# Gated linear attention followed by a maxout MoE: inputs of batches 1 to 3 loaded by one DMA per tensor and batch

## The chip, the cores and the metric

One core of one Trainium2 chip. The metric is the device time of one execution in microseconds (us). Each version ran several times; a run of the kernel before went with every group, on the same chip. Runs over 1.5% above the fastest run of the same kernel are set aside as slow; only fast runs are compared.

Engines go by the profile's names: PE is the tensor engine (matmuls), DVE the vector engine, ACT the scalar engine, POOL the GpSimd engine, SP the one that issues the input loads. The granted clock is the share of its full clock that PE was given, 1.00 at full clock.

## The reference

Two parts, cut to what matters here. Shapes: batch 4, 8 heads, sequence 768, head size 48, all in fp32.

```python
def _attn_ref(q, k, v, alpha):
    ...
    for t in range(S):
        state = alpha[:, :, t, :, None] * state + np.einsum('bhd,bhe->bhde', k[:, :, t], v[:, :, t])
        y[:, :, t] = np.einsum('bhd,bhde->bhe', q[:, :, t], state)
def _moe_ref(x, w1, w2, w_out):               # w1, w2: 384 x 1024, w_out: 1024 x 384
    h1 = x @ w1
    h2 = x @ w2
    g = np.maximum(h1, h2)
    return (g @ w_out).astype(np.float32)
# x is y with heads side by side: (batch * sequence, heads * head size) = 3072 x 384
```

## The kernel before

The sequence of each batch is cut into 6 chunks of 128 rows, so there are 24 chunks, 6 per batch. Chunk 6 is the first of batch 1, chunk 12 the first of batch 2, chunk 18 the first of batch 3. Each chunk needs four inputs of 192 KB (alpha, k, q, v: 128 partitions, 8 heads, 48 values of 4 bytes), and each came by its own DMA, two chunks ahead in the program:

```python
ldp = ctx.enter_context(tc.tile_pool(name="ldp", bufs=8))
def load(i):
    b, c = divmod(i, NCH)                     # NCH = 6, C = 128
    t = {}
    for name, src in (("af", alpha), ("kf", k), ("qf", q), ("vf", v)):
        t[name] = ldp.tile([128, H, D], FP32, tag=name, name=name)
        nc.sync.dma_start(out=t[name], in_=src[b, :, c * C : (c + 1) * C, :].rearrange("h p d -> p h d"))
    loads[i] = t
```

The chain of one chunk, by the names that the profile shows (`...` marks cuts):

```python
lg = Ln(af)                # ACT        vp = cast(vf)          # POOL
cs = mrec @ lg             # PE: decay sums
Em, Ep = exp(-cs), exp(cs) # ACT
kn = kf * Em               # POOL       qn = qf * Ep           # DVE
tp = transposes of kn, qn  # PE, 4 + 4  qk = copy(tp)          # DVE
kv = kn^T @ vp             # PE, 4      tm, sb: state          # DVE, POOL
pp = qk @ qk               # PE, 8      pt = pp * mask         # DVE
yp = sb, vp products       # PE, up to 16
...
# moe(w), for each window of two chunks, one window behind:
hp = w12 @ xt              # PE, 24     gT = relu(hp)          # ACT, DVE
op = w2o @ xt + wo @ gT    # PE, 22     outs -> DRAM           # ACT queue
```

The MoE matmuls (hp, op) do not depend on the chunk in work. (As max(h1, h2) is h2 + relu(h1 - h2), w12 holds w1 - w2, and w2o holds w2 times w_out, wo.) They are the filler for the holes that the chain leaves on the tensor engine. The program's scheduler fixes the order of each engine's instructions when the program is built; it decides by its own estimate of when the data will be there.

Of the kernel before, what the change touches and what calls it, by code (L numbers as in the profile page):

```python
# [9 lines left out]
FP32 = mybir.dt.float32  # L10
# [5 lines left out]
def kernel(  # L16
# [20 lines left out]
    nc = tc.nc  # L37
    B, H, S, D = q.shape
    C = 128
    NCH = S // C  # L40
    NI = B * NCH
    HP = H // 2
    P64 = 64
    NT, DM = out.shape
    DFF = moe_w1.shape[1]
    NF = DFF // 128
    ND = DM // 128
# [2 lines left out]

    constp = ctx.enter_context(tc.tile_pool(name="constp", bufs=1))
    wp = ctx.enter_context(tc.tile_pool(name="wp", bufs=1))
    ldp = ctx.enter_context(tc.tile_pool(name="ldp", bufs=8))
    gp = ctx.enter_context(tc.tile_pool(name="gp", bufs=3))
    mp = ctx.enter_context(tc.tile_pool(name="mp", bufs=2))
    psp = ctx.enter_context(tc.tile_pool(name="psp", bufs=1, space=bass.MemoryType.PSUM))

    nc.scalar.preload_act_table_set("natural_log_exp_and_others")

    loads = {}  # L60

    def load(i):
        b, c = divmod(i, NCH)
        t = {}
        for name, src in (("af", alpha), ("kf", k), ("qf", q), ("vf", v)):
            t[name] = ldp.tile([128, H, D], FP32, tag=name, name=name)
            nc.sync.dma_start(out=t[name], in_=src[b, :, c * C : (c + 1) * C, :].rearrange("h p d -> p h d"))
        loads[i] = t

    load(0)  # L70
    load(1)
    w2f = wp.tile([128, ND, DFF], FP32)
    wof = wp.tile([128, NF, DM], FP32)
    w1f = wp.tile([128, ND, DFF], FP32)
    nc.sync.dma_start(out=w2f, in_=moe_w2.rearrange("(s p) f -> p s f", p=128))
    nc.sync.dma_start(out=wof, in_=moe_w_out.rearrange("(s p) d -> p s d", p=128))
    nc.sync.dma_start(out=w1f, in_=moe_w1.rearrange("(s p) f -> p s f", p=128))
# [17 lines left out]
    for n in range(NB):  # L95
        for lst, nm in ((LG, "lg"), (QN, "qn"), (KN, "kn")):
            t = constp.tile([128, H, P64], FP16, name=f"{nm}{n}")
            nc.gpsimd.memset(t, 0.0)
            lst.append(t)
        t = constp.tile([128, 128 + H * VS], FP16, name=f"vp{n}")  # L100
# [3 lines left out]
    for n in range(3):  # L104
        t = constp.tile([128, 128 + HP * SS], FP16, name=f"sb{n}")
# [20 lines left out]
    def weights():  # L126
        for ds in range(ND):
            nc.scalar.copy(out=w2h[:, ds, :], in_=w2f[:, ds, :])
            wt = psp.tile([128, NF, 128], FP16, tag="m", bufs=3, name="wt")
            for f in range(NF):  # L130
                nc.tensor.transpose(wt[:, f, :], w2h[:, ds, f * 128 : (f + 1) * 128], ident)
            nc.vector.tensor_copy(out=w2T[:, :, ds * 128 : (ds + 1) * 128], in_=wt)
        nc.gpsimd.tensor_copy(out=wo16, in_=wof)
        for ds in range(ND):
            wq = psp.tile([128, DM], FP32, tag="m", bufs=3, name="wq")
            for f in range(NF):
                nc.tensor.matmul(
                    wq, lhsT=w2T[:, f, ds * 128 : (ds + 1) * 128], rhs=wo16[:, f, :],
                    start=(f == 0), stop=(f == NF - 1),
                )  # L140
            nc.scalar.copy(out=w2o[:, ds, :], in_=wq)
        for ds in range(ND):
            nc.vector.tensor_sub(out=w12[:, ds, :], in0=w1f[:, ds, :], in1=w2f[:, ds, :])
# [3 lines left out]

    def gla(i):
        b, c = divmod(i, NCH)
        t = loads.pop(i)  # L150
        lg, qn, kn, vp = LG[i % NB], QN[i % NB], KN[i % NB], VP[i % NB]
        vd = vp[:, 128:].rearrange("p (h w) -> p h w", w=VS)[:, :, 0:D]
        nc.scalar.activation(out=lg[:, :, 0:D], in_=t["af"], func=ACTF.Ln)
# [31 lines left out]
        if c:  # L185
# [5 lines left out]
            for a in range(2):  # L191
# [3 lines left out]
                    out=sd[r, :, e], in0=tm[r], in1=dd[r, :].unsqueeze(2).to_broadcast([64, HP, D])  # L195
# [24 lines left out]
        for a in range(2):  # L220
            nc.vector.tensor_mul(  # L221
                out=pt[:, a], in0=pa[a], in1=u16.unsqueeze(1).to_broadcast([128, HP, C])
# [10 lines left out]
        w = i // 2  # L233
# [4 lines left out]
    def moe(w):  # L238
        xt = xts.pop(w)
        gT = mp.tile([128, NF, 2 * C], FP16, tag="gT", name="gT")  # L240
        for f2 in range(NF // 2):
            hp = psp.tile([128, 2, 2 * C], FP32, tag="m", bufs=3, name="hp")
            for n in range(2):
                f = 2 * f2 + n
                for ds in range(ND):
                    nc.tensor.matmul(  # L246
                        hp[:, n, :], lhsT=w12[:, ds, f * 128 : (f + 1) * 128],
                        rhs=xt[:, ds].rearrange("p n t -> p (n t)"), start=(ds == 0), stop=(ds == ND - 1),
                    )
            if f2 % 2 == 0:  # L250
                nc.scalar.activation(out=gT[:, 2 * f2 : 2 * f2 + 2, :], in_=hp, func=ACTF.Relu)  # L251
            else:
                nc.vector.tensor_relu(out=gT[:, 2 * f2 : 2 * f2 + 2, :], in_=hp)  # L253
        outs = mp.tile([128, 2, DM], FP32, tag="outs", bufs=3, name="outs")
        for n in range(2):
            op = psp.tile([128, DM], FP32, tag="m", bufs=3, name="op")
            for ds in range(ND):
                nc.tensor.matmul(op, lhsT=xt[:, ds, n, :], rhs=w2o[:, ds, :], start=(ds == 0), stop=False)  # L258
            for f in range(NF):
                nc.tensor.matmul(  # L260
                    op, lhsT=gT[:, f, n * C : (n + 1) * C], rhs=wo16[:, f, :], start=False, stop=(f == NF - 1)
                )
            nc.scalar.copy(out=outs[:, n, :], in_=op)  # L263
        nc.scalar.dma_start(
            out=out[w * 2 * C : (w + 1) * 2 * C, :].rearrange("(n p) d -> p n d", p=C), in_=outs
        )

    LAG = 1
    NWIN = NI // 2
    for i in range(NI):  # L270
        if i + 2 < NI:
            load(i + 2)
        gla(i)
        if i == 1:
            weights()
        if i % 2 == 1 and i // 2 - LAG >= 0:
            moe(i // 2 - LAG)
    for w in range(NWIN - LAG, NWIN):
        moe(w)
# [30 lines left out]
```

## Time and profile before

| | kernel before |
|---|---|
| time, median of the three runs at hand then | 187.52 us (187.39 to 189.44) |
| span of the profiled execution | 185.5 us |
| packets of inputs | 98,304 of 192 B |
| mean granted clock of the tensor engine, profiled execution | 0.990 |

The page and its main rows stand in the prediction below. Two more rows: the slices of the page (40 of 4.64 us; a digit is the busy share in tenths) for the tensor engine and for its granted clock.

```profile
PE   0025779779887898896997878888878988969991
PEclk9999969999999999999999999999999999999999
```

The clock row has a 6 in slice 6, and is full (9) elsewhere. Read the same kernel in stretches of 3.41 us from 61 to 74.65 us; 3.41 us is the step in which the recorded clock changes in these traces (the kernel before: 0.50 from 24.66 to 28.07). (Columns: stretch, its length, busy time of PE with instructions, granted clock, mean share of the DMA engines, GB/s. A share over 1 means that the recorded times of packets overlap.)

```profile
61.00:64.41 3.41, 3.41 (x41) 1.00 0.58 116
64.41:67.83 3.42, 2.85 (x31) 1.00 1.41 195
67.83:71.24 3.41, 3.38 (x36) 1.00 1.15 154
71.24:74.65 3.41, 2.71 (x30) 1.00 1.06 256
```

Where batch 1 begins, PE is busy between 79% (2.71 of 3.41) and 100%, at full clock.

### The profile page before, as it was taken

The numbers are of one execution on the slowest core, as the hardware profiler recorded it, in microseconds if no ns is written. First come the engines' busy times: TensorE is split into PE (matmuls) and PEld (weight loads), VectorE is DVE, ScalarE is ACT, GpSimd is POOL, SyncE is SP. The second block draws the span as 40 slices with busy tenths as digits, with TensorE's granted clock in tenths as the row PEclk, the third lists the DMA queues.
The fourth block names the chain that finished last, engine by engine and source line by source line (L and its number), as shares of the span: only waits on it lengthen the run. The fifth ranks groups of instructions, "written<-read, shape, count | busy, mean of one in ns | idle before, by whom it ended". The sixth has DMA issues, their size and how long they took to land. (4 is left out here: it accounts for less than half of the span.)

```text
span 185.5 us, 3954 instructions
## 1 busy us (share of the span) xinstructions
PE 145.4 (78%) x1544; PEld 101.6 (55%) x1544; DVE 102.6 (55%) x175; ACT 73.8 (40%) x175; POOL 75.9 (41%) x129
## 2 busy tenths in 40 slices
PE   0025779779887898896997878888878988969991
PEld 0024637556555666564675555566556665646760
DVE  4122765782764962955926757717649529559220
ACT  3306306525454616426344443252455163253331
POOL 8950730661464245436512543523633353355000
PEclk9999969999999999999999999999999999999999
DMA  6999999999699599996999994997920020020022
GB/s 119 189 351 378 370 189 169 196 187 168 163 201 216 114 191 206 190 189 142 185 161 221 205 208 105 194 189 157 169 88 0 4 85 2 5 85 0 4 85 85
DMA packets 104963, 28.57 MB, mean 154 GB/s; under 512 B 100080, under 2 KB 104176, under 8 KB 104944
## 3 DMA queue, kind: packets, MB, share of 16 engines
q1 hardware_dynamic: 101680, 23.60, 73.7%
q10 hardware_dynamic: 3264, 4.72, 7.4%
q8 instruction: 12, 0.20, 0.5%
q14 instruction: 7, 0.06, 0.1%
HBM read 23.59 MB, written 4.72 MB: 153 GB/s over the span
## 5 line engine op out<-in xcount | busy, mean ns | idle before, releaser
L171 POOL TENSOR_TENSOR kn<-kf,Em 128x384 f16<-128x384 f32 x24 | 23.9, 995 | 79.2 <-ACT Em L167 59.4
L260 PE MATMUL op<-wo,gT 128*128 128x384 f16 x192 | 40.6, 326 | 0.0
L246 PE MATMUL hp<-xt,w 128*128 128x256 f16 x288 | 38.9, 272 | 1.7 <-ACT xt L236 1.1
L221 DVE TENSOR_TENSOR pt<-pp,u 128x512 f16<-128x512 f32 x48 | 30.9, 685 | 6.2 <-PE pp L219 5.7
L253 DVE TENSOR_SCALAR gT<-hp 128x512 f16<-128x512 f32 x24 | 16.4, 684 | 24.1 <-PE hp L246 24.0
L246 PEld LDWEIGHTS <-w 128*128 128x128 f16 x288 | 26.1, 97 | 5.9 <-issue 3.2
L172 DVE TENSOR_TENSOR qn<-qf,Ep 128x384 f16<-128x384 f32 x24 | 21.1, 878 | 14.1 <-ACT Ep L168 10.6
L232 PE MATMUL yp<-pt,vp 128*128 128x128 f16 x240 | 26.3, 223 | 1.1 <-DVE pt L221 0.8
L177 PE MATMUL tp<-ident,kn 128*128 128x128 f16 x96 | 10.7, 229 | 19.5 <-POOL kn L171 19.5
L263 ACT COPY outs<-op 128x384 f32<-128x384 f32 x24 | 11.5, 480 | 33.6 <-PE op L260 33.5
L181 DVE COPY qk<-tp 128x1024 f16<-128x1024 f16 x24 | 16.5, 689 | 14.3 <-PE tp L177 12.9
L260 PEld LDWEIGHTS <-gT 128*128 128x128 f16 x192 | 16.9, 97 | 9.9 <-issue 1.8
L251 ACT ACTIVATE gT<-hp 128x512 f16<-128x512 f32 x24 | 14.4, 602 | 18.3 <-PE hp L246 18.2
L194 POOL TENSOR_TENSOR sb<-tm,dd 64x192 f16<-64x192 f32 x40 | 20.3, 506 | 2.9
L177 PEld LDWEIGHTS <-kn 128*128 128x128 f16 x96 | 6.1, 100 | 26.0 <-POOL kn L171 26.0
L232 PEld LDWEIGHTS <-vp 128*128 128x128 f16 x240 | 18.2, 100 | 3.3 <-issue 0.2
L167 ACT ACTIVATE Em<-cs 128x384 f32<-128x384 f32 x24 | 11.8, 493 | 18.8 <-PE cs L161 18.8
L236 ACT CAST xt<-yp 128x384 f16<-128x384 f32 x24 | 11.5, 479 | 18.6 <-PE yp L232 17.3
L154 POOL CAST vp<-vf 128x384 f16<-128x384 f32 x24 | 13.1, 550 | 12.6 <-PE yp L232 9.1
L232 PE MATMUL yp<-qk,sb 128*128 128x128 f16 x120 | 16.8, 222 | 1.0 <-POOL sb L194 1.0
L258 PE MATMUL op<-w2o,xt 128*128 128x384 f16 x72 | 16.9, 325 | 0.0
L209 DVE TENSOR_TENSOR tm<-kv,sb 64x192 f32<-64x192 f32 x32 | 11.3, 352 | 5.7 <-POOL sb L194 5.0
(46 smaller groups left out, 161.4 us busy)
## 6 DMA issues: line engine op xcount, KB each, us to landing
af<-in_alpha_dram SPq DMA_DIRECT2D x24, 192.0 KB, 4.5
kf<-in_k_dram SPq DMA_DIRECT2D x24, 192.0 KB, 4.6
qf<-in_q_dram SPq DMA_DIRECT2D x24, 192.0 KB, 4.6
vf<-in_v_dram SPq DMA_DIRECT2D x24, 192.0 KB, 4.6
out_dram<-outs ACTq DMA_DIRECT2D x12, 384.0 KB, 3.4
w2f<-in_moe_w_dram SPq DMA_DIRECT2D x1, 1536.0 KB, 7.3
wof<-in_moe_w_out_dram SPq DMA_DIRECT2D x1, 1536.0 KB, 10.5
w1f<-in_moe_w_dram SPq DMA_DIRECT2D x1, 1536.0 KB, 14.0
```

Of the source, the lines that this page charges most:

```text
L171: nc.gpsimd.tensor_mul(out=kn[:, :, 0:D], in0=t["kf"], in1=Em)
L172: nc.vector.tensor_mul(out=qn[:, :, 0:D], in0=t["qf"], in1=Ep)
L177: nc.tensor.transpose(tp[:, n, j, :], src[:, 2 * j : 2 * j + 2, :].rearrange("p h w -> p (h w)"), ident)
L181: nc.vector.tensor_copy(out=qk, in_=tp)
L194: nc.gpsimd.tensor_mul(out=sd[r, :, e], in0=tm[r], in1=dd[r, :].unsqueeze(2).to_broadcast([64, HP, D]))
L221: nc.vector.tensor_mul(out=pt[:, a], in0=pa[a], in1=u16.unsqueeze(1).to_broadcast([128, HP, C]))
L232: nc.tensor.matmul(yp[:, ds, :], lhsT=l, rhs=r, start=(n == 0), stop=(n == len(mms) - 1))
L246: nc.tensor.matmul(hp[:, n, :], lhsT=w12[:, ds, f * 128 : (f + 1) * 128], rhs=xt[:, ds].rearrange("p n t -> p (n t)"), start=(ds == 0), st ...
L251: nc.scalar.activation(out=gT[:, 2 * f2 : 2 * f2 + 2, :], in_=hp, func=ACTF.Relu)
L253: nc.vector.tensor_relu(out=gT[:, 2 * f2 : 2 * f2 + 2, :], in_=hp)
L258: nc.tensor.matmul(op, lhsT=xt[:, ds, n, :], rhs=w2o[:, ds, :], start=(ds == 0), stop=False)
L260: nc.tensor.matmul(op, lhsT=gT[:, f, n * C : (n + 1) * C], rhs=wo16[:, f, :], start=False, stop=(f == NF - 1))
```

## The change

The intent: fewer and longer DMAs. Batch 0 is still loaded by chunks, because the first chunk should start early. For batches 1 to 3 there is one DMA per tensor and batch (1.1 MB). Each head's 48 values go to a slot of 64 values (256 B). Two buffers per tensor hold whole batches; the fp32 weights are staged in the same buffers, and one buffer of the working tiles is given up for the room (gp, three to two). The whole change:

```diff
--- before.py
+++ after.py
@@ -50,28 +50,36 @@
 
     constp = ctx.enter_context(tc.tile_pool(name="constp", bufs=1))
     wp = ctx.enter_context(tc.tile_pool(name="wp", bufs=1))
-    ldp = ctx.enter_context(tc.tile_pool(name="ldp", bufs=8))
-    gp = ctx.enter_context(tc.tile_pool(name="gp", bufs=3))
+    ldp = ctx.enter_context(tc.tile_pool(name="ldp", bufs=2))
+    gp = ctx.enter_context(tc.tile_pool(name="gp", bufs=2))
     mp = ctx.enter_context(tc.tile_pool(name="mp", bufs=2))
     psp = ctx.enter_context(tc.tile_pool(name="psp", bufs=1, space=bass.MemoryType.PSUM))
 
     nc.scalar.preload_act_table_set("natural_log_exp_and_others")
 
-    loads = {}
-
-    def load(i):
-        b, c = divmod(i, NCH)
-        t = {}
+    bt = {}
+
+    def load(b, c=None):
+
         for name, src in (("af", alpha), ("kf", k), ("qf", q), ("vf", v)):
-            t[name] = ldp.tile([128, H, D], FP32, tag=name, name=name)
-            nc.sync.dma_start(out=t[name], in_=src[b, :, c * C : (c + 1) * C, :].rearrange("h p d -> p h d"))
-        loads[i] = t
-
-    load(0)
-    load(1)
-    w2f = wp.tile([128, ND, DFF], FP32)
-    wof = wp.tile([128, NF, DM], FP32)
-    w1f = wp.tile([128, ND, DFF], FP32)
+            if (name, b) not in bt:
+                bt[name, b] = ldp.tile([128, H, NCH, P64], FP32, tag=name, name=name)
+            t = bt[name, b]
+            if c is None:
+                nc.sync.dma_start(
+                    out=t.rearrange("p h c w -> p (h c) w")[:, :, 0:D],
+                    in_=src[b].rearrange("h (c p) d -> p (h c) d", p=C),
+                )
+            else:
+                nc.sync.dma_start(
+                    out=t[:, :, c, 0:D], in_=src[b, :, c * C : (c + 1) * C, :].rearrange("h p d -> p h d")
+                )
+
+    load(0, 0)
+    load(0, 1)
+    w2f = ldp.tile([128, ND, DFF], FP32, tag="qf", name="w2f")
+    wof = ldp.tile([128, NF, DM], FP32, tag="kf", name="wof")
+    w1f = ldp.tile([128, ND, DFF], FP32, tag="af", name="w1f")
     nc.sync.dma_start(out=w2f, in_=moe_w2.rearrange("(s p) f -> p s f", p=128))
     nc.sync.dma_start(out=wof, in_=moe_w_out.rearrange("(s p) d -> p s d", p=128))
     nc.sync.dma_start(out=w1f, in_=moe_w1.rearrange("(s p) f -> p s f", p=128))
@@ -147,7 +155,7 @@
 
     def gla(i):
         b, c = divmod(i, NCH)
-        t = loads.pop(i)
+        t = {n: bt[n, b][:, :, c, 0:D] for n in ("af", "kf", "qf", "vf")}
         lg, qn, kn, vp = LG[i % NB], QN[i % NB], KN[i % NB], VP[i % NB]
         vd = vp[:, 128:].rearrange("p (h w) -> p h w", w=VS)[:, :, 0:D]
         nc.scalar.activation(out=lg[:, :, 0:D], in_=t["af"], func=ACTF.Ln)
@@ -265,11 +273,13 @@
             out=out[w * 2 * C : (w + 1) * 2 * C, :].rearrange("(n p) d -> p n d", p=C), in_=outs
         )
 
+    for c in range(2, NCH):
+        load(0, c)
     LAG = 1
     NWIN = NI // 2
     for i in range(NI):
-        if i + 2 < NI:
-            load(i + 2)
+        if i % NCH == 0 and i // NCH + 1 < B:
+            load(i // NCH + 1)
         gla(i)
         if i == 1:
             weights()
```

## The prediction

> **What bounds the kernel now.** I read the page's head and slices first, to see which engine is full and where, then the waits, to see who waits for data from memory, then the stretches, then the timeline around the seventh chunk (chunk 6, the first of batch 1), because the change moves what that chunk waits for.
>
> The page of the kernel before (engines; then the DMA rows over 40 slices of 4.64 us; then the issues):
>
> ```profile
> span 185.5 us, 3954 instructions
> PE 145.4 (78%) x1544; PEld 101.6 (55%) x1544; DVE 102.6 (55%) x175; ACT 73.8 (40%) x175; POOL 75.9 (41%) x129
> ...
> DMA  6999999999699599996999994997920020020022
> GB/s 119 189 351 378 370 189 169 196 187 168 163 201 216 114 191 206 190 189 142 185 161 221 205 208 105 194 189 157 169 88 0 4 85 2 5 85 0 4 85 85
> DMA packets 104963, 28.57 MB, mean 154 GB/s; under 512 B 100080, under 2 KB 104176, under 8 KB 104944
> ...
> vf<-in_v_dram SPq DMA_DIRECT2D x24, 192.0 KB, 4.6
> ```
>
> The DMA engines are full until slice 30 but move only about 190 GB/s, half of what they do in the slices with the weights (351 to 378): nearly all packets are the 192 B rows of the inputs. That looks like a DMA bound. The waits say it is not:
>
> ```profile
> PE tp L177 <- POOL kn L171: 19.5, 21, 6.2
> ...
> ACT w2h L128 <- DMA w2f<-in_moe_w_dram: 6.3, 1, 6.3
> ...
> ACT lg L153 <- DMA af<-in_alpha_dram: 4.0, 2, 2.0
> ```
>
> A compute engine waits for a DMA three times in all (columns: us in total, times, longest), all at the start: two Ln of chunks 0 and 1 and the first weight. After 15 us nobody waits for an input. What waits is the queue itself, on the completion counters that loads share with output stores and on chunk buffers:
>
> ```profile
> SPq L67 <- DMA out_dram<-outs: 25.1, 7, 4.9
> ```
>
> And the stretch of steady work:
>
> ```profile
> 31.00:60.00 29.00, 24.56 (x275) 17.17 (x273) 16.29 (x28) 13.08 (x33) 13.76 (x24) 1.00 1.15 190
> ```
>
> PE is busy 24.56 of 29 us, at full clock. So the middle is bound by PE, plus the chain of one chunk (decay sums, Em, kn on POOL, transposes, qk, scores, pt, y) wherever there is no MoE matmul to fill its holes. The order of every engine's queue is fixed when the program is built: where the filler stands decides the time.
>
> The timeline around the end of batch 0's loads (start, duration):
>
> ```profile
> 35.70 0.99 SPq L67 DMA_DIRECT2D vf<-in_v_dram  x1
> 36.74 1.00 SPq L67 DMA_DIRECT2D af<-in_alpha_dram  x1
> 37.78 0.99 SPq L67 DMA_DIRECT2D kf<-in_k_dram  x1
> 38.82 1.00 SPq L67 DMA_DIRECT2D qf<-in_q_dram  x1
> ...
> 57.87 0.99 POOL L171 TENSOR_TENSOR kn<-kf,Em 128x384 f16<-128x384 f32 x1 [2.69 <-ACT Em L167]
> 58.81 0.95 POOL L154 CAST vp<-vf 128x384 f16<-128x384 f32 x2
> 59.80 0.54 DVE L172 TENSOR_TENSOR qn<-qf,Ep 128x384 f16<-128x384 f32 x1
> ```
>
> The row at 35.70 is v of chunk 5, the last load of batch 0. The next one is alpha of chunk 6. A full queue takes one 192 KB load per 1.04 us (36.74 to 37.78 to 38.82). The lower three rows are where chunk 6 uses k and q (57.87, 59.80), and where v is cast for later chunks; its own v cast was at 54.68. So with one DMA per chunk, chunk 6's inputs, landing by about 45, were ten microseconds early.
>
> [...] each load releases its chunk once, 4.6 us after issue. [...] half of the 98,304 packets of 192 B take 15 ns, and in the first load of alpha nearly all do, whatever their place in the row. So I expect no gain from alignment.
>
> **The change part by part.**
> 1. Issues: 96 loads become 24 for batch 0 and 12 large ones. SP computes nothing, so fewer issues are worth nothing by themselves. The counter waits of 25.1 us on SP go away too; no compute engine waited behind them, so they are worth 0.
> 2. Bytes and packets: the same 98,304 packets of 192 B. Rate: 1.04 us per 192 KB with a full queue, so 6.2 us per large DMA (six chunks) and 25 us for the four of a batch.
> 3. When batch 1 lands. The queue reaches it at 36.7 as before. Its buffers, which held the weights, are free by then (the last weight subtraction on DVE ends at 30.1). The last loads of batch 0 land at 35.7 + 4.6 = 40.3. Then, in queue order: alpha 46.5, k 52.7, q 58.9, v 65.1; plus about 1 us for each of the two output stores that come between, by 393 KB at the 378 GB/s of the weights' slices: q about 60.5, v about 67. Before, chunk 6 cast its v at 54.68: v comes 12 us later.
> 4. The static order. The built program shows that the scheduler knows of the late batch: in the new PE queue all of the MoE of chunks 4 and 5 (24 hp matmuls and 14 of 22 op) stands ahead of chunk 6's transposes, 5 more op between those of kn and qn, and chunks 6 and 7 run without filler. Before, this filler was spread over chunks 6 and 7. So PE does not simply stand still 12 us.
> 5. Sum, walked with durations of the trace before. cs of chunk 6 at about 57.7; 24 hp (24 x 0.115 us apart = 2.8) and 14 op (0.163 apart = 2.3), with evictions, to 64.2; transposes and 5 op to 65.8; qk (0.69) and pp to 67. kv of chunk 6 waits for v: 67 + 0.5 cast = 67.6. From there chain only: yp of chunk 6 ends about 69.5; cs (0.5), Em (0.5), kn (1.0), tp (0.8), qk with tm (1.0), pp (0.4), pt (1.3) and yp put chunk 8's decay sums near 74, chunk 9's near 79.5; the end of chunk 9 and the last 17 op come to 90. In the trace before, the same set of work (chunks 0 to 9, MoE of windows 0 to 3) is done at 83.4. That is 6.5 us late. The other limit: after 67.6 PE has about 19 us of work left in that set (kv and yp of chunk 6, three chunks of 3.6 us, one MoE of 6.3 us); packed without a hole it ends at 86.6, 3.2 us late. I take 5.5 us, nearer to the walk, because a chunk without filler leaves holes.
> 6. Batches 2 and 3: their buffers come free with chunk 5 (52 to 55) and chunk 11; batch 2 lands by about 97 with chunk 12 wanting v near 100; batch 3 starts near 95 to 100, lands by 125, and is wanted about 10 us later. No further wait. Two gp buffers for three: each user is done a chunk before the buffer comes round; 0.
> 7. Start, per-instruction times and tail: unchanged. The inputs are read with another stride between heads but the same 48 contiguous values.
>
> Sum: 187.5 + 5.5 = 193.0.
>
> **Rivals.** (a) Hidden: if the reordered MoE fills the wait fully and the later order is as dense, the loss is 3 us or less and the kernel stays within 2%. For it: PE has 8 us of filler put just there. Against it: the filler is then missing in chunk 7. (b) The large DMA is slower per packet (48 scattered rows per partition, slots with gaps, output stores between). If it took 20 ns per packet (the mean of all packet records, against 16 from the pace) v lands near 74 and the kernel takes about 200. (c) Aligned slots or longer DMAs make it faster, the 15 ns floor: v at 65; that gains at most 1 to 2 us, since the order is static, and gives about 192. (d) A gain over before: the queue runs ahead earlier; but nobody waited for it, so I see no mechanism.
>
> **Range and chances.** From 3 us (PE packed) to 10 us (slower packets with some filler): 189.5 to 198. The 2% line is 191.3, below my middle by 1.7 and inside the range, so slower 0.70, within 2% 0.26, faster 0.04.
>
> **What would show it.** Right: the first casts or multiplies of chunk 6 wait for a DMA (POOL vp on vf, by some microseconds, landing near 67); PE busy time unchanged at 145; a dip of PE between 60 and 80; the rest shifted by a constant; large loads landing 6 us apart. Wrong: no wait for vf and yet slower (order alone); waits at chunks 12 or 18 (buffers come free too late); packets clearly slower or faster than 16 ns at a full queue; longer kn, qn, lg or vp from the new stride.

## The result and the profile after

| | before, same rounds | after |
|---|---|---|
| median (range, fast runs) | 188.06 us (187.39 to 189.44, 4) | 203.16 us (202.18 to 203.44, 4) |
| ratio of means | 1 | 1.0783, 95% interval 1.0706 to 1.0861 |
| mean granted clock, profiled execution | 0.990 | 0.947 |
| span, profiled execution | 185.5 us | 200.1 us |

A ratio here is the mean time of one kernel's fast runs over the mean of the other's fast runs of the same rounds, so it is not quite the ratio of the medians. The change costs 15.1 us. Slower was the likelier outcome in the prediction, but 203.16 lies outside its range (189.5 to 198.0).

The head of the page after, with the rows of the engine slices (5.0 us each) and the packets:

```profile
span 200.1 us, 3842 instructions
...
PE 150.4 (75%) x1544; PEld 105.9 (53%) x1544; DVE 103.1 (52%) x175; ACT 73.9 (37%) x175; POOL 75.5 (38%) x129
...
PE   0025679788989635689889888896897877988890
...
PEclk9999957999999985589999999999999999999999
...
DMA packets 48705, 28.55 MB, mean 143 GB/s; under 512 B 25392, under 2 KB 47920, under 8 KB 48688
```

Three things to see. The PE row has one dip, at slices 14 to 17 (65 to 85 us): digits 6, 3, 5, 6. The clock row has a second dip at the same place, which the kernel before has not. And there are half as many packets: the records hold 24,576 packets of 192 B (batch 0) and 18,432 of 768 B, so in the large loads, by the sizes, four rows of 192 B make one packet. The folded packets carry 192 B in 18.8 ns on average (75.2 ns / 4), the single ones of batch 0 now take 22.9 ns, and in the kernel before a packet of 192 B took 20.0 ns. These are times of single packets; what rate comes of them is looked at under e3_contig.

Who waits for a DMA after (us in total, times, longest):

```profile
POOL vp L162 <- DMA vf<-in_v_dram: 11.4, 2, 10.2
ACT w2h L136 <- DMA w2f<-in_moe_w_dram: 6.8, 1, 6.8
ACT lg L161 <- DMA af<-in_alpha_dram: 4.8, 2, 2.7
DVE qn L180 <- DMA qf<-in_q_dram: 3.9, 2, 3.6
```

The first and the last row are new. The last is at the start: chunk 0 waits 3.6 us for q, as it does in e1_slots below (3.4). The first: the cast of v waits 10.2 us once. This is the wait that the prediction named. The timeline shows where (start, duration; in brackets the idle time before it and who ended it):

```profile
68.92 0.40 PE L227 MATMUL pp<-qk 48*128 48x128 f16 x8 [0.79 <-DVE qk L189]
...
72.78 1.40 POOL L162 CAST vp<-vf 128x384 f16<-128x384 f32 x3 [10.16 <-DMA vf<-in_v_dram]
73.33 0.48 PE L208 MATMUL kv<-vp,kn 128*128 128x96 f16 x4 [4.02 <-POOL vp L162]
...
75.89 0.99 POOL L179 TENSOR_TENSOR kn<-kf,Em 128x384 f16<-128x384 f32 x1 [0.37 <-ACT Em L175]
```

The filler is used up at 67.9, chunk 6's last matmul before kv (pp) ends at 69.3, and PE stands still for 4.02 us until v of chunk 6 has been cast. kn of chunk 7 begins at 75.89; before, it began at 63.8. The stretches of 3.41 us, in the same columns as above:

```profile
66.29:69.71 3.42, 2.24 (x25) 1.00 1.13 164
69.71:73.12 3.41, 0.00 (x0) 1.00 1.09 245
73.12:76.53 3.41, 1.95 (x19) 0.50 1.12 186
76.53:79.95 3.42, 2.22 (x23) 0.50 0.96 164
79.95:83.36 3.41, 1.89 (x19) 0.50 1.13 167
83.36:86.77 3.41, 3.41 (x31) 0.50 1.09 158
86.77:90.18 3.41, 2.65 (x38) 1.00 1.12 168
```

After the empty stretch the granted clock was 0.50 for four stretches (73.12 to 86.77); in the last of them PE was full. Where the time is lost along the kernel, by the start of kn in each chunk, after minus before (one trace each): +1.3 us at chunk 1, +2.6 at chunks 2 to 5, +3.8 at chunk 6, +12.0 at chunk 7, 13.2 at chunk 10, 14.3 at chunk 23 (13.9 at chunk 11 already, and 9.7 to 14.0 in the others from chunk 8 on, as the orders differ). So 2.6 us arise at the start and nearly all the rest once, at the border between batch 0 and batch 1; batches 2 and 3 add well under 1 us.

### The profile page after: what moved, and what is told of

Its sections match the earlier page's. It is cut to its first block, busy times and chain, and to the rows that moved or that the text cites. A ratio compares the mean times of both kernels' runs of the same rounds, so it can differ in the third digit from the quotient of the medians.

```text
span 200.1 us, 3842 instructions
## 1 busy us (share of the span) xinstructions
PE 150.4 (75%) x1544; PEld 105.9 (53%) x1544; DVE 103.1 (52%) x175; ACT 73.9 (37%) x175; POOL 75.5 (38%) x129
## 2 busy tenths in 40 slices
DMA packets 48705, 28.55 MB, mean 143 GB/s; under 512 B 25392, under 2 KB 47920, under 8 KB 48688
## 4 chain that ended last, share of the span: by engine, by line
PE 40%; POOL 16%; DMA 12%; issue 9%; SPq 7%; ACT 7%; DVE 6%; POOLq 0%; ACTq 0%; DVEq 0%
PE yp L240 8%; PE op L268 8%; DMA vf<-in_v_dram 8%; POOL kn L179 7%; PE hp L254 6%; ACT Em L175 4%; POOL sb L202 4%; PE tp L185 4%; DMA w2f<-in_moe_w_dram 4%; SPq L69 4%; SPq L74 4%; PE op L266 4%; PE pp L227 3%; PE wq L145 3%; DVE pt L229 2%
## 5 line engine op out<-in xcount | busy, mean ns | idle before, releaser
L268 PE MATMUL op<-wo,gT 128*128 128x384 f16 x192 | 40.1, 326 | 0.0
L180 DVE TENSOR_TENSOR qn<-qf,Ep 128x384 f16<-128x384 f32 x24 | 21.3, 886 | 15.7 <-ACT Ep L176 11.5
L240 PE MATMUL yp<-pt,vp 128*128 128x128 f16 x240 | 28.1, 234 | 1.1 <-DVE pt L229 0.8
L185 PE MATMUL tp<-ident,kn 128*128 128x128 f16 x96 | 11.3, 232 | 21.2 <-POOL kn L179 21.2
L240 PEld LDWEIGHTS <-vp 128*128 128x128 f16 x240 | 19.5, 106 | 3.7 <-issue 1.1
L240 PE MATMUL yp<-qk,sb 128*128 128x128 f16 x120 | 17.5, 230 | 1.0 <-POOL sb L202 1.0
L161 ACT ACTIVATE lg<-af 128x384 f16<-128x384 f32 x24 | 12.7, 532 | 4.8 <-DMA af<-in_alpha_dram 4.8
## 6 DMA issues: line engine op xcount, KB each, us to landing
w1f<-in_moe_w_dram SPq DMA_DIRECT2D x1, 1536.0 KB, 14.3
```

Of the source, the lines that this page charges most:

```text
L180: nc.vector.tensor_mul(out=qn[:, :, 0:D], in0=t["qf"], in1=Ep)
L185: nc.tensor.transpose(tp[:, n, j, :], src[:, 2 * j : 2 * j + 2, :].rearrange("p h w -> p (h w)"), ident)
L240: nc.tensor.matmul(yp[:, ds, :], lhsT=l, rhs=r, start=(n == 0), stop=(n == len(mms) - 1))
L268: nc.tensor.matmul(op, lhsT=gT[:, f, n * C : (n + 1) * C], rhs=wo16[:, f, :], start=False, stop=(f == NF - 1))
```

## The experiments

The theory after the first look: (T1) the large loads deliver chunk 6's v too late; (T2) the 256 B slots make each load slower; (T3) the built order, which has spent the filler ahead of chunk 6, makes the rest late; (T4) the half clock adds to it. Rivals: the third gp buffer, the staging of the weights, or the large DMA as such.

The built order of PE's matmuls around chunks 6 to 8 (cs begins a chunk; number of matmuls after the star; this is the program's order, not a trace):

```
before      [6] cs*5 yp*13 tp*4 kv*4 hp*9 tp*4 hp*8 pp*8 hp*7 yp*1
            [7] cs*5 op*2 yp*9 op*2 tp*8 kv*4 op*4 pp*8 yp*2 op*4 yp*1 op*4 yp*13 op*6
after       [6] cs*5 hp*24 op*17 tp*4 op*5 tp*4 pp*8 kv*4 yp*10
            [7] cs*5 tp*4 kv*4 tp*4 pp*8 yp*2
e7_bigrows  [6] cs*5 yp*13 tp*4 hp*14 tp*4 hp*9 pp*8 hp*1 op*9 kv*4 yp*10
            [7] cs*5 op*7 tp*4 kv*4 tp*4 op*6 pp*8 yp*2
```

### The slots alone: the kernel before with 256 B slots (e1_slots)

```diff
-            t[name] = ldp.tile([128, H, D], FP32, tag=name, name=name)
+            tt = ldp.tile([128, H, P64], FP32, tag=name, name=name)
+            t[name] = tt[:, :, 0:D]
```

> The kernel before, with one part of the change: each chunk's load goes into slots of 256 B (192 B written) instead of contiguous 1536 B rows. Order on every engine as before. Theory P (the slots make a full queue slower, 1.04 to about 1.17 us per 192 KB load, seen in the changed kernel's loads of batch 0): pace 1.13 to 1.18 us, first weight 1.3 us later, chunk 2's kn near 35 instead of 32.4, total 189.5 to 191. Rival (the 1536 B distance between heads or the large tile causes it, or the chip's state): pace 1.04, total as before, 187.5 to 188.5. In neither case does a compute engine wait for a load after chunk 1.

Measured: 188.65 us (187.10 to 188.72), ratio 1.0008 (0.9951 to 1.0066): the same. But the loads are slower. Its DMA view (the input queue's share, then size and median us from issue to landing):

```profile
q1 hardware_dynamic: 101680, 23.60, 84.2%
...
af<-in_alpha_dram SPq DMA_DIRECT2D x24, 192.0 KB, 5.3
kf<-in_k_dram SPq DMA_DIRECT2D x24, 192.0 KB, 5.3
```

Before, this queue took 73.7% and the loads landed after 4.5 and 4.6 us. The packets are 192 B in both; their mean time in the records is 23.1 ns here, 20.0 before. The queue reaches batch 1 at 40.37 instead of 36.74. So the pace came as the theory had it, but the total that it gave (189.5 to 191) did not: slots cost transfer time, and by themselves no kernel time that shows. With one DMA per chunk there is slack to hide it, if not much: contrary to both expectations POOL waits for a load twice later on (3.0 us for v at 83.2, 2.8 us at 109.4), and neither wait moves the start of a kn (0.2 to 0.3 us early in every chunk from 2 on).

### Batch 1 by chunks (e2_b1chunks)

```diff
         if i % NCH == 0 and i // NCH + 1 < B:
-            load(i // NCH + 1)
+            if i // NCH + 1 == 1:
+                for c in range(NCH):
+                    load(1, c)
+            else:
+                load(i // NCH + 1)
```

> The changed kernel with batch 1 alone loaded by chunks again (slots, gp of 2, staged weights and whole batches 2 and 3 kept). Theory B (nearly all of the loss is batch 1 arriving as one piece: order made for it, wait for v, half clock after it): no wait for v at chunk 6, no half clock near 73, total 189.5 to 191.5, that is the 2.6 us of the first 35 us and little else. Rival (staging, gp of 2 or the large batches 2 and 3 cost too): above 193, with a wait or a jump of the lag at chunk 12 or 18.

Measured: 192.62 us (192.33 to 193.41), ratio 1.0246 (1.0197 to 1.0295). Some 10 of the 15 us are gone, so that much hangs on batch 1 coming as one piece. The built order changed with it, so the wait (T1) and the order (T3) are not told apart here. The total lies between the two expected ranges, and what is left turned up one batch later. At chunk 12 the same picture as in the kernel after at chunk 6 (POOL timeline; then stretches of PE in the columns of before):

```profile
105.79 1.41 POOL L162 CAST vp<-vf 128x384 f16<-128x384 f32 x3 [6.27 <-DMA vf<-in_v_dram]
```

```profile
104.38:107.80 3.42, 2.82 (x35) 1.00 1.02 242
107.80:111.21 3.41, 0.81 (x12) 1.00 1.13 166
111.21:114.62 3.41, 1.78 (x18) 0.50 1.10 255
```

The start of kn is 1.2 us late up to chunk 12 and 4.3 us late at chunk 13. So the second border is no safer than the first; in the kernel after, batch 2 is in time because everything already runs 12 us late (its v lands at 101.7, and kn of chunk 12 begins at 109.6).

### Large loads without slots (e3_contig)

```diff
-                bt[name, b] = ldp.tile([128, H, NCH, P64], FP32, tag=name, name=name)
+                bt[name, b] = ldp.tile([128, H, NCH, D], FP32, tag=name, name=name)
```

> The changed kernel with contiguous slots of 192 B instead of 256 B; the order on all four engines is the same, instruction by instruction. Theory P: loads of batch 0 at 1.04 us again, large loads at 6.2 instead of 7 us, packets of 192 B again, v of batch 1 lands near 67 to 68 instead of 72.8, PE stands idle under 1 us before kv of chunk 6, half clock shorter or gone; total 193 to 197 (193.0 was the prediction with just this pace). Rival (large loads are slow because of their size, whatever the slots): v still near 71 to 73, total 200 to 203.

Measured: 196.29 us (195.59 to 197.72), ratio 1.0460 (1.0387 to 1.0532). The order of instructions is that of the kernel after on every engine, so the difference is the slots': 203.16 - 196.29 = 6.9 us by the medians, 6.1 us by the ratios (0.0323 of 188). The packet counts are the same as after (48,705 in all), so the folding of four rows comes from the whole-batch access, not from the slots. The mean packet times now stand in a square:

| | one row, 192 B | four rows, 768 B |
|---|---|---|
| no slots | 20.0 ns (before), 19.6 (e3_contig) | 64.8 ns (e3_contig), 16.2 per row |
| slots of 256 B | 23.1 ns (e1_slots), 22.9 (after) | 75.2 ns (after), 18.8 per row |

By these times slots cost 16% in both columns (75.2 / 64.8, and 23.1 / 20.0) and folding saves 19% in both lines (16.2 against 20.0, 18.8 against 23.1). But packets overlap, so their times are not rates. Four stretches without output stores, in the columns of before: chunk loads of the kernel before, large loads of e3_contig, chunk loads and large loads of the kernel after.

```profile
34.00:42.00 8.00, 6.85 (x84) 1.00 1.41 190
38.00:44.00 6.00, 5.42 (x65) 1.00 1.19 183
34.00:40.00 6.00, 4.96 (x58) 1.00 1.00 164
42.00:48.00 6.00, 5.60 (x64) 1.00 1.02 168
```

In GB/s the slots cost 14% (164 against 190) and 8% (168 against 183), and folding gains nothing that shows (183 against 190, 168 against 164). The landings say the same: the first large load lands 6.14 us after the load ahead of it without slots and 6.96 us with them, and six chunk loads of the kernel before, 1.05 us apart, take 6.3. Where the 6.9 us come from is in the queue. The kernel after (last chunk load of batch 0, then the four large loads; start and duration of the issue):

```profile
39.16 1.12 SPq L74 DMA_DIRECT2D vf<-in_v_dram  x1
40.49 0.99 SPq L69 DMA_DIRECT2D af<-in_alpha_dram  x1
41.93 6.34 SPq L69 DMA_DIRECT2D kf<-in_k_dram  x1
48.72 6.85 SPq L69 DMA_DIRECT2D qf<-in_q_dram  x1
56.03 6.71 SPq L69 DMA_DIRECT2D vf<-in_v_dram  x1
```

The same without slots, with the cast of v and the matmuls that it lets go:

```profile
36.65 1.00 SPq L69 DMA_DIRECT2D af<-in_alpha_dram  x1
...
51.87 6.36 SPq L69 DMA_DIRECT2D vf<-in_v_dram  x1
```

```profile
67.30 1.40 POOL L162 CAST vp<-vf 128x384 f16<-128x384 f32 x3 [7.24 <-DMA vf<-in_v_dram]
67.86 0.33 PE L208 MATMUL kv<-vp,kn 128*128 128x96 f16 x4 [1.09 <-POOL vp L162]
```

With slots the queue reaches batch 1 at 40.49, without at 36.65 (before: 36.74): 3.8 us, made in batch 0's own chunk loads (e1_slots, with the same slots and the old order, is there at 40.37). The large loads add 1.6: v is cast at 72.78 against 67.30, 5.5 us in all. The prediction had said "about 67" for v: right without slots. PE then stands still 1.09 us instead of 4.02. Still the kernel is 8.4 us slower than before (196.29 - 187.87), and the half clock is there too, in the three stretches from 69.11:

```profile
65.70:69.11 3.41, 1.58 (x27) 1.00 1.04 196
69.11:72.53 3.42, 1.36 (x12) 0.50 1.10 221
72.53:75.94 3.41, 1.60 (x16) 0.50 1.11 247
75.94:79.35 3.41, 3.25 (x29) 0.50 0.81 146
```

### Three gp buffers again (e4_gp3)

```diff
-    gp = ctx.enter_context(tc.tile_pool(name="gp", bufs=2))
+    gp = ctx.enter_context(tc.tile_pool(name="gp", bufs=3))
```

> The changed kernel with three gp buffers again instead of two, nothing else; same order on all engines. The prediction gave the two buffers a cost of 0. If right: 202.5 to 203.5, lag of each chunk as in the changed kernel within the spread of its start-up half clock (0 to 3 us). Rival: if the missing third buffer makes Ln/Exp or qk wait in the stretch of chunks 7 to 9, 199 to 201.

Measured: 202.98 us (202.59 to 203.73), ratio 1.0823 (1.0761 to 1.0885), within the run-to-run spread of the kernel after. The lost buffer costs nothing that shows.

### No slots, and batch 1 by chunks (e5_contig_b1chunks)

The edits of e3_contig and e2_b1chunks together.

> Contiguous slots (as in e3) and batch 1 by chunks (as in e2), batches 2 and 3 still whole: both found costs taken away. The run with 256 B slots lost 3 to 4 us at chunk 12 by waiting 6.3 us for v of batch 2, which landed at 105.8. With the faster pace (5.5 to 6.5 instead of 6.4 to 7.9 us per large load, and nothing late at the start) v of batch 2 should land at 95 to 98. Theory (time of arrival is all that counts): wait at chunk 12 under 1 us, no half clock near 111, total 187.5 to 189. Rival (a whole batch is late again for batch 2 even so): wait of 2 us or more there, 190 to 192.

Measured: 192.14 us (191.36 to 193.37), ratio 1.0262 (1.0181 to 1.0342). A miss: it is no faster than with slots. The wait at chunk 12 is gone (v is waited for 0.5 us in the whole kernel), yet kn of chunk 13 begins 3.3 us late, against 0.3 at chunk 12. What is left there is the order, which has a window's MoE ahead of the state matmuls (kv) of chunk 12 and none in chunk 13, and two stretches of half clock from 110.66:

```profile
107.25:110.66 3.41, 1.10 (x20) 1.00 1.10 191
110.66:114.08 3.42, 1.91 (x20) 0.50 1.05 267
```

So the built order is paid for even when the data comes in time (T3): kn of chunk 13 begins at 107.29, before the clock falls. How much the half clock adds (T4) is not told apart here.

### More scores in chunk 6, against the half clock (e6_fill6 and e6b_1_8)

In the kernel after, chunk 6's 8 score matmuls are done 6 times instead of once ahead of pt (e6_fill6), or 8 times more behind pt (e6b_1_8), writing the same values again, so that PE is busy while v is on its way.

```diff
-        for j in range(HP):
+        for j in [j for _ in range(6 if i == 6 else 1) for j in range(HP)]:      # e6_fill6
             for a in range(2):
                 r = slice(64 * a, 64 * a + D)
                 nc.tensor.matmul(pa[a][:, j, :], lhsT=qk[r, 1, j, :], rhs=qk[r, 0, j, :], start=True, stop=True)
 ...
+        for j in [j for _ in range(8 if i == 6 else 0) for j in range(HP)]:      # e6b_1_8, behind pt
+            ... the same four lines
```

> The changed kernel with the score matmuls of chunk 6 done six times instead of once (the same result), 40 more small matmuls, some 2.1 us of PE work in the 4.0 us in which PE stands idle before kv of chunk 6. Order else the same on PE, DVE and ACT. Theory C (the idle stretch brings 13.65 us of half clock, which costs 3 to 5 us): with idle shortened to about 2 us the half clock is gone or shorter, chunk 8's kn comes 1 to 3 us earlier than 81.2, total 198 to 201. Rival (the chain of one chunk, not the clock, sets the pace there): clock back to 1.0 but total within 1 us of 203; or the clock drops all the same.

> Second try at the clock. In the first, 40 extra small matmuls took 1.5 us in all, ended where the plain kernel's work ended, and v landed 0.8 us later, so PE was idle 4.8 us all the same and the half clock came (17.1 us): it told nothing apart. Here some 60 repeated score matmuls stand behind the masking of chunk 6 on DVE, to keep PE busy from about 70.7 to 72.6 us, with no gap over 1.5 us before kv. If the idle stretch is what brings the half clock: clock 1.0 from 70 to 87, or half for at most 3.4 us, chunks 8 and 9 earlier by 1 to 4 us, total 199 to 202. If the clock drops all the same, the low load of the chain without filler brings it (three chunks with PE half idle), and the total stays near 203.

Measured: 202.16 us (201.53 to 203.06), ratio 1.0750 (1.0695 to 1.0805), and 203.33 us (202.38 to 203.69), ratio 1.0829 (1.0767 to 1.0891). Both failed to keep the clock: it went to half at 71.2 and at 71.4. In the first the 48 small matmuls took only 1.5 us. In the second the stretch before was 68% busy, and the clock fell all the same:

```profile
67.95:71.36 3.41, 2.33 (x61) 1.00 1.11 164
71.36:74.78 3.42, 1.16 (x19) 0.50 1.10 261
```

These matmuls use 48 of 128 rows. They say nothing about what the half clock costs, so that was tried again, in e8_filled.

### The same large DMAs with long rows (e7_bigrows)

The version without slots, each batch read as contiguous rows of 9,216 B. The values land in the wrong places, so the result is wrong (relative error 1.01); the work is the same.

```diff
-                    out=t.rearrange("p h c w -> p (h c) w")[:, :, 0:D],
-                    in_=src[b].rearrange("h (c p) d -> p (h c) d", p=C),
+                    out=t.rearrange("p h c w -> p (h c w)"),
+                    in_=src[b].rearrange("h (g r) d -> (h g) (r d)", r=H * NCH),
```

> Wrong result on purpose: the whole batches 1 to 3 are read as 9216 B contiguous rows into contiguous slots (the same bytes and the same number of DMAs, other rows than the kernel needs). Theory (the loss comes from when batch 1 lands, not from one DMA per tensor as such): loads at 350 to 400 GB/s, 3.1 to 3.6 us each, v of batch 1 lands near 53 to 56, no wait for it, no half clock near 70; the built order differs a little from both; total 186.5 to 189.5. Rival (large DMAs cost through their granularity or their order alone): 191 or more without any wait.

Measured: 188.40 us (188.26 to 188.62), ratio 1.0042 (0.9990 to 1.0094). The page row of rates (40 slices of 4.67 us) and the one row that waits for v:

```profile
GB/s 123 192 345 378 368 200 158 198 305 416 423 351 410 345 16 220 132 240 84 28 406 159 0 88 0 4 84 0 4 84 2 25 63 2 4 84 0 87 1 84
...
POOL vp L162 <- DMA vf<-in_v_dram: 0.2, 1, 0.2
```

The same bytes come at 305 to 423 GB/s (slices 9 to 14) instead of 183 to 252 in the same slices of e3_contig, v is there, and the clock stays full outside the start and the end. So one DMA per tensor and batch is not slow as such; what differs from e3_contig in these loads is the rows, 9,216 B instead of 192 B. Its order is near that of the kernel after but not equal (13 op remain in chunk 7, as listed above), so it does not price that order by itself.

### The holes filled with full-size matmuls (e8_filled)

The version without slots, with extra matmuls into a spare PSUM tile that nobody reads. The order up to chunk 8 is that of e3_contig.

```diff
+    FILL = {7: (6, 7, 3), 8: (4, 0, 3)}          # chunk: how many of each kind
 ...
+        n1, n2, n3 = FILL.get(i, (0, 0, 0))
+            for m in range(n1): matmul(fl[m % 2][:, 0 : H * D], lhsT=mrec, rhs=lg[:, :, 0:D])    # 128x384
+            for m in range(n2): matmul(fl[m % 2], lhsT=mrec, rhs=vp[:, 128:640])                 # 128x512
 ... after the transposes:
+            for m in range(n3): matmul(fl[m % 2], lhsT=kn[:, 0:2, :], rhs=qn)                    # 128x512
```

> The version with contiguous slots (e3_contig, 196.29 us), with extra full-size matmuls whose results nobody reads put into the holes of the tensor engine around chunks 6 to 8: 6 of 128x384 before kv of chunk 6, 7 of 128x512 between the decay sums and the transposes of chunk 7, 3 of 128x512 after them, 7 more around chunk 8. The MoE order up to chunk 8 is that of e3_contig. [...] Theory (the chunks without filler load PE too little, the half clock follows from that and costs about 3 us of the 8.4 us that are left in e3_contig): no half clock in 60 to 90 us, total 193 to 194.5 us. Rival A (the half clock costs nothing, because the chain is bound by ACT, POOL and DVE): no half clock and 196 us or more. Rival B (the clock does not follow the busy share): half clock near 69 us again, 196 to 198 us.

Measured: 195.31 us (194.82 to 195.91, 6 fast runs), ratio 1.0391 (1.0336 to 1.0446). The clock stayed full:

```profile
66.08:69.50 3.42, 2.04 (x26) 1.00 1.08 211
69.50:72.91 3.41, 3.12 (x28) 1.00 1.10 246
72.91:76.32 3.41, 2.17 (x27) 1.00 1.10 218
```

So with PE loaded more the half clock was gone here: the stretch with 60% (2.04 of 3.42) was followed by full clock, where in e3_contig the one with 46% (1.58 of 3.41) was followed by 0.50. But the gain is small. The ratio falls by 0.0069, 1.3 us of 188, less than the 2 us or more that was expected; the two intervals overlap a little and the runs are from different calls. It is a net figure: the filler itself holds up kn of chunk 7 by 1 us (70.8 against 69.8), and from there to kn of chunk 10 it takes 19.9 us instead of 21.3. So the 1.3 us are uncertain: the medians as they stand differ by 1.0 us (196.29 - 195.31), each taken against its own kernel before by 1.9 (8.42 against 6.57). As the theory had it, there was no half clock between 60 and 90 us with the holes filled; on its price the theory was too high; rival A, that it costs nothing, had expected 196 us or more.

One half-clock stretch more takes 3.41 x 0.5 / 187 = 0.009 off the mean clock. In the kernel before, fast runs with a mean clock of 0.998 had a mean span of 184.4 us (2 runs), with 0.989 to 0.991 186.0 us (13), with 0.982 186.9 us (6): 0.9 to 1.6 us for each stretch. That is a correlation, not a test: something else may be late in those runs and lower the clock too.

### Batches 1 and 2 by chunks, only batch 3 large (e9_b12chunks)

```diff
-            load(i // NCH + 1)
+            if i // NCH + 1 in (1, 2):
+                for c in range(NCH):
+                    load(i // NCH + 1, c)
+            else:
+                load(i // NCH + 1)
```

on the version without slots.

> Contiguous slots, batches 1 and 2 by chunks, only batch 3 by one DMA per tensor. The built order is that of the kernel before up to chunk 12. Theory (each batch that comes by large DMAs costs one stretch of order without filler, which later delays can hide but not undo): chunks 6 and 12 as before, a loss only at chunk 18: 189 to 192 us, and a stretch of half clock after 140 us if the two chunks behind the border stand without filler. Rival (by then the queue is far enough ahead that the third border costs nothing): 187.5 to 188.5 us, no half clock between 30 and 180 us.

Measured: 188.67 us (187.27 to 189.95), ratio 1.0027 (0.9960 to 1.0094): no difference from the kernel before that the runs show, close to what the rival expected. Of the kernel before, four runs of this call (which also served e8_filled) count as slow and are left out: one of 286.76 us, and three of 189.11 to 189.43 us that are just over 1.5% above the fastest one, 186.06. With these three kept in, the mean of the kernel before would be 0.4 us higher, and both ratios 0.002 lower. The clock row has only the dip at the start:

```profile
PEclk9999966999999999999999999999999999999999
```

This version still has the weights in the load buffers, two gp buffers, and one border with large loads. So neither the staging nor the buffers cost anything that shows, and at the third border, by the built order, the scheduler keeps filler between the transposes of chunk 18 (hp*8), as the kernel before does (hp*9 with kv*4 ahead of them). No version here beats the kernel before; nothing in the experiments points to one, since the kernel before has no wait for an input after its start.

## Why the prediction was right or wrong

- **Issues and counter waits (step 1).** Right. SP's waits on the output stores before loads (25.1 us) are gone, and nothing got faster.
- **Packets and pace (step 2).** "The same 98,304 packets of 192 B" was wrong: the large loads have 18,432 packets of 768 B. But the rate that the prediction took from the old packets held for the large loads without slots (183 against 190 GB/s in e3_contig): the folding shortens the packets' recorded times by 19% per row and gains no rate that shows. The slots do cost rate (168 GB/s).
- **When batch 1 lands (step 3).** This is the step that failed. It used the old pace, 1.04 us per chunk load, for loads into slots. Measured pace with slots: about 1.16 (35.51 to 36.67 to 37.82 in the kernel after; 1.11 to 1.18 in e1_slots), and 6.96 us between landings for the first large load instead of 6.2. The prediction had looked for an effect of alignment only as a gain ("So I expect no gain from alignment"); that slots with gaps could cost came only in rival (b), and there in the large DMAs. The aligned slots did not merely fail to gain, they cost, and first in batch 0: the queue was 3.8 us late before the first large load, and v came at 72.8 instead of 67. e3_contig, with v at 67.30 and the same built order, prices this at 6.9 us of the kernel (6.1 by the ratios).
- **The static order (step 4).** Right in kind, with one misreading: 17 op matmuls, not 14, stand ahead of chunk 6's transposes, so with the 5 between them all 22 are spent. e5_contig_b1chunks shows that such an order costs 3 us at a border without a real wait.
- **The sum (step 5).** With v where the prediction put it (e3_contig) the loss is 8.4 us, not 5.5. The walk itself came out: there chunk 8's decay sums begin at 73.7 ("near 74"), chunk 9's at 80.2 ("near 79.5"), and the last of the 17 op ends at 90.1 ("come to 90"). That is partly luck, since three half-clock stretches lie in it, which no step had; e8_filled, with the clock full and its own filler in the way, is at the same point at 89.8. What was too low came behind the walk: 5.5 was taken where it gave 6.5, and the rest, up to 2 us, shows only later: at chunk 10 its decay sums are 7.5 us late and its kn 6.6, the profiled spans differ by 8.0 and the medians by 8.4. No run tests where that comes from. For the four stretches of half clock in the kernel after there is no direct price: e6_fill6 and e6b_1_8 failed. An estimate from e8_filled's 1.3 us net for three stretches is about 2 us, one from the 0.9 to 1.6 us per stretch in the kernel before is 4 to 6. A part of it would be in the 6.9 us of the slots, as e3_contig has three of these stretches and the kernel after four.
- **Batches 2 and 3 (step 6).** "No further wait" came true, but for a reason that was not in it: the kernel was 12 us late by then. With batch 1 in time, e2_b1chunks waited 6.27 us for v of batch 2. "Two gp buffers cost 0" is confirmed by e4_gp3.
- **Start and tail (step 7).** The start was not unchanged: kn of chunk 2 began 2.6 us late in the kernel after. Two things stand there: the chunk loads into slots (kn of chunk 1 is 1.3 us late, 1.1 in e1_slots, which had made it good by chunk 2), and a half-clock stretch at 25 us of 6.8 us instead of 3.4 (e9_b12chunks, without slots, has the same long stretch and is 1.7 us late at chunk 2).
- **The rivals.** Rival (b), "about 200", was the nearest: v "near 74" against 72.8 measured. That was partly luck; it had the size but not the place: it put 20 ns on the packets of the large DMAs, which took 18.8 per row, and none on batch 0's, which took 22.9. Rival (a), hidden, and (c), a gain from slots or longer DMAs, fell, and (d), faster than before, fell too. (The 15 ns in (c) is what half of the old packet records show, no floor: 1,086 of the 98,304 are shorter.)
- **The early start.** The large DMA took it away (v of chunk 6 was cast at 72.78 instead of 54.68), and with rows of 192 B it gave no rate in return (183 against 190 GB/s in e3_contig).
- **The half clock.** No step of the prediction has it. In the traces of the kernels before and after, the recorded clock has two values, 1.00 and 0.50, in stretches that are multiples of 3.41 us, but for the last one of a trace. An idle stretch was not needed: in e3_contig the stretch before the half clock was 46% busy (1.58 of 3.41) and its longest wait of PE was 1.09 us. Of the full-clock stretches that were read, these were followed by half clock: 0% busy (0.00 of 3.41) and 48% (1.64 of 3.41) in the kernel after, 38% (1.29 of 3.41) in the kernel before, 24% (0.81 of 3.41) in e2_b1chunks, 32% (1.10 of 3.41) in e5_contig_b1chunks, and 68% (2.33 of 3.41) in e6b_1_8, with matmuls of 48 rows. These were not: 60% (2.04 of 3.42) and 64% (2.17 of 3.41) in e8_filled. Half-clock stretches of 65% (2.22 of 3.42) and 71% (2.41 of 3.41) in the kernel after were followed by another one; those of 87% (2.98 of 3.41) in the kernel before, 95% (3.25 of 3.41) in e3_contig and 100% (3.41 of 3.41) in the kernel after by full clock. No run tests where a limit lies.

What stays open: how the 8.4 us of e3_contig divide between the built order and the wait, as loading by chunks or reading long rows also changed the order; and how much of the slots' 6.9 us passes through the clock.

## What to carry to other kernels

Read the slack before merging loads: one DMA per chunk released chunk 6's data ten microseconds early (v landed by about 45 and was cast at 54.68), and a DMA per batch released it only with the last chunk's (v, issued at 56.03, could be cast at 72.78). If the rows in memory stay short, a longer DMA may gain no rate, as here (183 against 190 GB/s without slots); compare the bytes moved per time in stretches without other traffic, not the number of packets nor their recorded times, which overlap (their sum came to 1.41 of the DMA engines' time), and do so for the destination's layout too, since gaps there cost rate here (164 against 190 GB/s, 168 against 183). And where filler is spent ahead of a late transfer, look at the busy share of PE in the stretches that follow, because the clock may fall too (here to 0.50, after stretches with PE 0% and 46% busy).
